# Attention plus token/channel mixer on one core: leftover tokens on all 128 rows, and a scheduler with two transfer queues and new priorities

## The chip, the cores and the metric

The kernel runs on one core of a Trainium2 chip. The metric is the device time of one execution in microseconds (us), the median of three runs. Five engines work in parallel, each on its own list of instructions, in order: PE (TensorE, matrix products), DVE (VectorE), ACT (ScalarE), POOL (GpSimd) and SP (SyncE, which here only issues DMA transfers). ACT issues transfers too. Engines wait for each other through semaphores.

## The reference, cut to what matters

```python
# batch 4, 8 heads, 576 tokens, head size 64; mixer: 576 tokens, 512 channels
scores = q @ k.T / 8 + bias            # bias: per head, from log1p(|i-j|) / log1p(max(i,1)) through
                                       # a hidden layer of 32: relu(x @ w1 + b1) @ w2
attn   = exp(scores - max); attn /= sum(attn) + 1e-9
x      = attn @ v                      # laid out [batch, 576 tokens, 512 channels]
u      = x + (relu(x.T @ w_tok1) @ w_tok2).T       # mixing over tokens, 576 -> 256 -> 576
out    = u + relu(u @ w_ch1) @ w_ch2               # mixing over channels, 512 -> 1536 -> 512
```

## The kernel before

A "unit" is one pair of heads of one batch: 16 units, each 128 channels wide. The 576 query tokens of a unit are cut into four chunks of 128 and 64 **leftover** tokens, which are the fifth chunk (`c == NCH`, `NCH` is 4). In the fifth chunk both heads stand in one tile, head 0 in rows 0 to 63 and head 1 in rows 64 to 127.

PE's steps are these. `mm` (L441) makes one of 36 blocks of the bias, with 32 rows out. `sums` (L474) are 8 small products over v. Per unit there are then nine score products (`scores`, L666, which contract over 64 rows, q by k; the leftover one has 64 rows in and 64 out), nine `flip` transposes (L703), five `back` products (L746 to L748, probabilities by v, in three terms of half precision, 30 instructions), and the token mixer `mix1` (L796 to L798) and `mix2` (L805 to L807), 30 instructions each. After the units come 60 products `chan1` (L968 to L970) and 54 `chan2` (L998 to L1000) of the channel mixer.

In the fifth chunk `back` loads weights of 64 columns for each head, `w[h]`, and writes both heads into the same 64 rows `r`: rows 0 to 63 for an even batch, 64 to 127 for an odd one. The leftover tokens of a unit are therefore a 64 x 128 piece of the tile `x`. `mix1` contracts over these 64 rows in its fifth part (`p = r`), twice (t = 0 and 1); `mix2` makes their result as a product with 64 columns of weights (`slice(512, S)`), at its end.

Between these steps: DVE adds the bias to scores and takes the maximum (`biased`, L670), ACT takes the exponential (L684), flipped blocks are split into two half-precision numbers by ACT (`flip_hi`, L706) and DVE (`flip_lo`, L710), the rest is split by ACT and POOL and turned by a DMA transpose (L722, issued by SP). There are two score buffers (`pair`) and four other PSUM buffers (`bank`). Weights are stored as 64-bit words and are decoded piece by piece (`decode`, L548): DVE, POOL, ACT, DVE.

The order on every engine is not written by hand. Each step is added to a `Plan` with a cost per engine and a due time, made of `BASE`, `TICK` and the table `DUE`; `order()` (L178) picks the engine that can begin first and on it, among the steps that could begin within `SLACK`, the one with the earliest due time. Transfers go to SP's list ("D") or to ACT's ("Q"), and the planner knows one common wire on which they follow each other.

Of the kernel before, what the change touches and what calls it, by code (L numbers as in the profile page):

```python
# [36 lines left out]
TICK = 2.35  # L37
BASE = 67.64
# [16 lines left out]
DUE = {'blk': 29.05,  # L55
       'blkn': 0.67,
       'rect': -81.27,
       'bmm': -146.83,
       'over': -7.76,
       'put': -41.17,  # L60
       'bl': -22.15,
       'bln': 15.56,
       'sums': -79.57,
       'sumsn': 0.87,
       'meas': -52.82,
       'measn': -1.79,
       'measw': 98.18,
       'measwn': 6.48,
       'amax': 56.12,
       'scales': 48.16,  # L70
       'scalet': -63.64,
       'scalec': -167.78,
       'fill': 239.74,
       'fill1': 213.34,
       'tok': 90.83,
       'tokn': 2.6,
       'dec1': 47.92,
       'dec2': -2.25,
       'dec3': -65.12,
       'dec4': 33.12,  # L80
       'dec5': -14.78,
       'load_k': -23.79,
       'load_q': 70.61,
       'load_v': -135.93,
       'prep_k': -68.51,
       'prep_kl': -48.97,
       'prep_q': 82.92,
       'prep_ql': 1.69,
       'prep_v': -126.84,
       'prep_vh': -4.6,  # L90
       'prep_vl': 125.82,
       'scores': 26.19,
       'biased': 82.41,
       'top': 2.07,
       'exp': -41.11,
       'hi': -98.5,
       'lo': -23.53,
       'flip': 29.87,
       'fliphi': 24.58,
       'flip2': 1.74,  # L100
       'fliplo': 11.27,
       'turn': -7.48,
       'back': -24.67,
       'norm': 83.98,
       'mix0': -57.52,
       'mix1': 39.31,
       'relu': -78.51,
       'mix2': -80.52,
       'mix2b': -120.9,
       'store': 48.6,  # L110
       'w1': 22.4,
       'w1n': 11.84,
       'U0': -13.72,
       'U0n': -3.2,
       'U1n': -19.84,
       'U1': -42.9,
       'U2': 133.32,
       'Un': 3.09,
       'U3': 35.03,
       'U4': 250.78,  # L120
       'u1': -106.99,
       'u2': -102.94,
       'u3': 58.75,
       'u4': 8.97,
       'u5': 73.75,
       'G': 114.15,
       'G0': 71.27,
       'G0n': 7.22,
       'g1': -6.35,
       'g2': 90.55,  # L130
       'ur': 190.4,
       'w2m': 20.95,
       'w2mn': 5.39}
# [9 lines left out]
class Step:  # L143
# [5 lines left out]
    def __init__(self, on, due, do, take, free, use, port):  # L149
        key = next(iter(on))  # L150
        self.wire, self.gate = (on[key] if key in "DQX" else 0.0), key == "X"
        on = {"Q": {"A": 0.1}, "X": {"D": 0.0}, "D": {"D": 0.0}}.get(key, on)
# [7 lines left out]
class Plan:  # L160
# [5 lines left out]
    def add(self, on, due, do, after=(), take=(), free=(), use=(), port=False):  # L166

        s = Step(on, due, do, take, free, use, port)
        for p in after:
            if p is not None:  # L170
                p.next.append(s)
                s.left += 1
        for h in free:
            h.users += 1
        self.steps.append(s)
        return s

    def order(self):  # L178
        room = {k: [(0.0, i) for i in range(n)] for k, n in self.rooms.items()}
        at = {"V": 6.9, "A": 6.8, "P": 4.3, "T": 8.0, "D": 2.1, "-": 0.0}  # L180
        made = wire = port = 0.0
# [10 lines left out]
        while len(out) < len(self.steps):  # L192
            best = None
            for e, steps in ready.items():
                first, can = None, []
                for s in steps:
                    t = max(at[e], s.ready, *(h.busy[0] + (0.0 if h.busy[1] == e else 0.15) for h in s.bank))
# [23 lines left out]
            cost = s.on[e]  # L221
            s.start, s.engine = t, e
            if s.wire:
                made = max(made, t + 0.07) + 0.62
# [25 lines left out]
def attention_mixer(ctx, tc, qT, kT, v, cst, lg, ident, wt1, wt2, wc1, wc2, out, dump=None):  # L250
# [67 lines left out]
    def wire(kind, cost):  # L318

        return {QUEUE.get(kind, "D"): cost}  # L320
# [799 lines left out]
```

## Time and profile before

| | us |
|---|---|
| three runs | 712.43, 710.39, 712.82 |
| median | 712.43 |
| span of the profiled execution | 709.6 |
| PE busy in it | 660.5 |
| DVE busy | 469.2 |
| ACT busy | 375.0 |

The span runs from the first to the last instruction; the median run is 2.8 us longer than the profiled span. The execution falls into three stretches: the bias blocks with the first unit, up to about 105 us; the other 15 units, up to about 435; then the channel mixer. The last product ends at about 704.8.

How to read a time line: "start, duration, engine, line, operation, out<-in, shape". Matrix products overlap in PE's pipeline, so the cost of one is the distance from its start to the next one's start. A shape such as 64*128 on PE is the rows by columns of the weights.

### The profile page before, as it was taken

Reading aid. Unit: us, or ns where it says so; the run is one execution under the profiler, and the core shown is the slowest. Engines: PE = TensorE matmul, PEld = TensorE weight load, DVE = VectorE, ACT = ScalarE, POOL = GpSimd, SP = SyncE. Lnnn points to the kernel's source line nnn. Section 1 sums busy time; section 2 is a strip of 40 time slices with the busy share of each in tenths; the row PEclk is TensorE's granted clock in tenths of the full one; section 3 lists DMA queues with packets and bytes.
Section 4 is the critical chain, followed back from the end, with each engine's and each line's share of the span. In section 5 each row is a group of like instructions: output and inputs, shape, how many; then the busy total and the mean of one; then the engine's idle time right before and its main releaser. Section 6 shows DMA issues by size and latency. Waiting matters only on the chain. (4 is left out here: it accounts for less than half of the span.)

```text
span 709.6 us, 16671 instructions
## 1 busy us (share of the span) xinstructions
PE 660.5 (93%) x6612; PEld 391.8 (55%) x6612; DVE 469.2 (66%) x1164; ACT 375.0 (53%) x726; POOL 162.9 (23%) x226
## 2 busy tenths in 40 slices
PE   5776779999999999999999999999999999999997
PEld 2322246676667767776767776444444444446443
DVE  5788788987889999999898777579851022112110
ACT  4667769766787787777877653345531022012010
POOL 0121025332354544453323100013430000000000
PEclk9999999999999999999999999999999999999999
DMA  9878867889756596644452248967623220121021
GB/s 337 332 253 284 280 232 224 245 232 242 237 153 181 132 260 182 177 122 115 135 117 61 49 99 213 296 178 183 181 55 120 60 59 1 29 62 29 19 85 31
DMA packets 86814, 111.42 MB, mean 157 GB/s; under 512 B 46928, under 2 KB 56400, under 8 KB 86736
## 3 DMA queue, kind: packets, MB, share of 16 engines
q1 hardware_dynamic: 72048, 70.90, 35.6%
q10 hardware_dynamic: 14688, 39.46, 17.5%
q8 instruction: 52, 0.85, 0.5%
q14 instruction: 26, 0.21, 0.1%
HBM read 80.31 MB, written 20.05 MB: 141 GB/s over the span
## 5 line engine op out<-in xcount | busy, mean ns | idle before, releaser
L666 PE MATMUL pair<-kk,qq 64*128 64x288 f32 (+1 forms) x640 | 107.6, 454 | 8.6 <-DVE mx L670 5.9
L684 ACT ACTIVATE z<-z,mx 128x576 f32<-128x576 f32 x144 | 110.3, 775 | 6.4 <-DVE mx L691 2.6
L670 DVE CUSTOM_DVE_ANT_0 z<-pair,slots 128x576 f32<-128x576 f32 x144 | 108.4, 757 | 7.6 <-PE pair L666 6.2
L710 DVE TENSOR_TENSOR t2a<-bank,t2a 128x512 f16<-128x512 f32 x144 | 98.3, 687 | 16.4 <-ACT t2a L706 16.0
L706 ACT ACTIVATE t2a<-bank 128x512 f16<-128x512 f32 x144 | 84.4, 588 | 42.3 <-PE bank L703 35.6
L703 PE MATMUL bank<-id,z 128*128 128x128 f32 x576 | 92.7, 285 | 4.6 <-ACT z L684 2.9
L1009 DVE SCALAR_TENSOR_TENSOR o<-bank,crow,ur 128x512 f32<-128x512 f32 x18 | 13.5, 751 | 104.2 <-PE bank L1000 104.2
L703 PEld LDWEIGHTS bank<-id,z 128*128 128x128 f32 x576 | 60.8, 141 | 36.8 <-issue 13.6
L746 PE MATMUL bank<-vh,t2a 128*128 128x65 f16 (+1 forms) x704 | 75.7, 196 | 0.7 <-ACT t2a L706 0.7
L746 PEld LDWEIGHTS <-t2a 128*128 128x128 f16 (+1 forms) x704 | 65.0, 99 | 19.6 <-issue 12.3
L747 PE MATMUL bank<-vl,t2a 128*128 128x64 f16 (+1 forms) x704 | 75.0, 193 | 0.0
L748 PE MATMUL bank<-vh,t2a 128*128 128x65 f16 (+1 forms) x704 | 74.6, 194 | 0.0
L968 PE MATMUL bank<-slots 128*128 128x384 f16 (+1 forms) x192 | 67.8, 353 | 0.8 <-DVE t2a L710 0.8
L323 POOL TENSOR_TENSOR p<-z,p 128x128 f16<-128x128 f32 x80 | 36.6, 459 | 138.1 <-ACT p L308 111.5
L970 PE MATMUL bank<-slots 128*128 128x384 f16 (+1 forms) x192 | 67.7, 353 | 0.0
L969 PE MATMUL bank<-slots 128*128 128x384 f16 (+1 forms) x192 | 67.7, 353 | 0.0
L747 PEld LDWEIGHTS <-t2a 128*128 128x128 f16 (+1 forms) x704 | 65.8, 101 | 1.0 <-issue 0.8
L748 PEld LDWEIGHTS <-t2a 128*128 128x128 f16 (+1 forms) x704 | 65.9, 100 | 0.1
L441 PE MATMUL pair<-slots 128*32 128x288 f32 x576 | 48.5, 455 | 14.6 <-ACT slots L447 13.6
L425 DVE TENSOR_SCALAR slots<-slots 128x576 f32<-128x576 f32 x108 | 51.9, 548 | 15.1 <-PE pair L441 14.9
L666 PEld LDWEIGHTS pair<-kk,qq 64*128 64x128 f32 (+1 forms) x640 | 42.8, 175 | 33.8 <-issue 12.4
L990 ACT ACTIVATE ur<-ur,sc 128x512 f32<-128x512 f32 x18 | 13.0, 720 | 79.2 <-DMA ur<-um 65.1
(171 smaller groups left out, 1404.5 us busy)
## 6 DMA issues: line engine op xcount, KB each, us to landing
raw<-wc SPq DMA_DIRECT2D x48, 512.0 KB, 4.4
bd<-slots ACTq DMA_DIRECT2D x36, 288.0 KB, 4.0
kk<-kT ACTq DMA_DIRECT2D x16, 576.0 KB, 5.1
qq<-qT ACTq DMA_DIRECT2D x16, 576.0 KB, 5.9
slots<-bd SPq DMA_DIRECT2D x16, 576.0 KB, 6.1
tv<-v ACTq DMA_DIRECT2D x16, 320.0 KB, 3.6
slots<-v SPq DMA_DIRECT2D x8, 640.0 KB, 11.6
um<-x SPq DMA_DIRECT2D x16, 256.0 KB, 3.4
```

The costliest lines, as they stand in the source:

```text
L666: PE.matmul(out=o[:, n, 0:i], lhsT=qq[w, q0:q0 + m], rhs=kk[w, k0:k0 + i], start=True, stop=True)
L670: V.tensor_tensor_reduce(out=st["z"][z.i][:, o].rearrange("p (n j) -> p n j", n=2), in0=pairs[ph.i][:, :, 0:i], in1=(bias_m[hp][:, c, h, : ...
L684: A.activation(out=zz, in_=zz, func=ACTF.Exp, bias=mx_t[z.i][:, 2 + h:3 + h], scale=0.125)
L703: PE.transpose(banks[tb.i][:, n * 128:(n + 1) * 128], st["z"][z.i][:, 512 * i + n * 128:512 * i + (n + 1) * 128], id32)
L706: A.activation(out=st["t2a"][h.i][:, 0:4].rearrange("p n q -> p (n q)"), in_=banks[tb.i], func=ACTF.Copy)
L710: V.tensor_tensor(out=x[:, 512:1024], in0=banks[tb.i], in1=x[:, 0:512], op=ALU.subtract)
L746: PE.matmul(out=o, lhsT=lh, rhs=vh[:, n, 0:D + 1], start=(i == 0), stop=False)
L747: PE.matmul(out=ps[q, h, 0:D], lhsT=lh, rhs=vl[:, n, :], start=False, stop=False)
L748: PE.matmul(out=o, lhsT=ll, rhs=vh[:, n, 0:D + 1], start=False, stop=(i == 4))
L968: PE.matmul(out=ps[:, 0:n], lhsT=w[0][:, c], rhs=uh[:, c], start=(c == 0), stop=False)
L969: PE.matmul(out=ps[:, 0:n], lhsT=w[0][:, c], rhs=ul[:, c], start=False, stop=False)
L970: PE.matmul(out=ps[:, 0:n], lhsT=w[1][:, c], rhs=uh[:, c], start=False, stop=(c == 3))
```

## The change

First, the leftover tokens. `back` uses all 128 columns of the fifth chunk's weights for both heads and writes 128 rows; the useful part is block-diagonal (rows 0 to 63 with head 0's channels, rows 64 to 127 with head 1's), and only these two blocks are copied into `x`, whose other blocks stay zero. `mix1` contracts over all 128 rows, and `mix2` makes 128 columns: the second weights of the token mixer get their last 64 columns twice (640 instead of 576). On DVE the leftover normalisation and the leftover sum become two instructions of 64 x 64 where there was one of 64 x 128, and the leftover result of a unit is stored by two transfers of 64 x 64.

Second, the planner. It has two transfer queues ("A" and "D") that each keep their order and share bandwidth (`HALF`), with a work time, a lag and an issue time for each kind of transfer; steps on PE have a `mode`, and a change of mode costs `DRAIN`; some PE costs are lower. Third, `DUE`, `TICK` and `BASE` have other values throughout, so all engines get another order.

```diff
-TICK = 2.35
-BASE = 67.64
+DRAIN = 0.095
+HEAD, HALF, AHEAD = 1.2, 0.445, 2.0
+DMA = {"put": (1.06, 1.62, 0.35), ... "store_l": (0.56, 1.4, 1.0), "turn": (1.22, 1.56, 1.2), ...}
+ROWS64, ROWS64X2, COLS32 = ("64x128", 0.1), ("64x64", 0.1), ("128x32", 0.1)
+TICK = 4.659
+BASE = 5.791
-DUE = {'blk': 29.05,
+DUE = {'blk': -592.583,
...
+                    if e == "T" and s.mode != mode:
+                        t = max(t, at[e] + DRAIN)
...
             if s.wire:
-                made = max(made, t + 0.07) + 0.62
-                wire = max(wire, made + (0.65 if e == "D" else 0.78)) + s.wire
-                s.end = wire + 0.94
+                o = "D" if e == "A" else "A"
+                first = max(till[e], t + HEAD)
+                both = max(0.0, min(till[o] - first, s.wire / HALF))
+                till[e] = first + s.wire + both * (1.0 - HALF)
+                till[o] += both * (1.0 - HALF)
+                s.end = till[e] + s.lag - HEAD
...
                     if c < NCH:
-                        q = slice(0, 128)
                         blk = [[(n, n) for n in range(5)], [(n + 1, n) for n in range(4, 9)]]
-                        w = [slice(0, 128)] * 2
                     else:
-                        q = r
                         blk = [[(n + 5 * h, n) for n in range(5)] for h in range(2)]
-                        w = [slice(0, 64), slice(64, 128)]
...
-                            PE.matmul(out=o, lhsT=lh, rhs=vh[:, n, 0:D + 1], start=(i == 0), stop=False)
+                            PE.matmul(out=o, lhsT=th[t], rhs=vh[:, n, 0:D + 1], start=(i == 0), stop=False)
...
+                    elif c == NCH:
+                        for h, w in enumerate(half):
+                            V.tensor_scalar(out=xo[w, 0, h], in0=ps[w, 0, h, 0:D], scalar1=rc[w, 0, h], scalar2=None, op0=ALU.mult)
...
-                        p = slice(0, 128) if c < 4 else r
-                        PE.matmul(out=ps[:, t], lhsT=w1h[p, c, w], rhs=xh[p, c], start=(c == 0), stop=False)
+                        PE.matmul(out=ps[:, t], lhsT=w1h[:, c, w], rhs=xh[:, c], start=(c == 0), stop=False)
...
-                for o, w in [(ps[:, s], slice(s * 128, (s + 1) * 128)) for s in range(4)] + [(pl, slice(512, S))]:
+                for o, w in [(ps[:, s], slice(s * 128, (s + 1) * 128)) for s in range(4)] + [(pl, slice(512, 640))]:
...
+            def mixed_left(e):
+                for h, w in enumerate(half):
+                    o = x()[w, 4, 64 * h:64 * h + 64]
+                    V.scalar_tensor_tensor(out=o, in0=banks[b1.i][w, 256 + 64 * h:320 + 64 * h], scalar=c_tm[w], in1=o, op0=ALU.mult, op1=ALU.add)
+
+            def store_left(e):
+                for h, w in enumerate(half):
+                    ENG[e].dma_start(out=u_l[b // 2][r, hp * 128 + 64 * h:hp * 128 + 64 * h + 64], in_=x()[w, 4, 64 * h:64 * h + 64])
```

Three places show how the order moves. On PE, at the border of unit 1 and unit 2 (`pair` is a score buffer, `kk` and `qq` the keys and queries, a score of the fifth chunk is the one with 64x320; a row with `id32` is a flip). Before:

```order
L703 MATMUL bank2_68<-id32_73,z2_122 128x128 x4
L666 MATMUL pair0_64<-kk1_107,qq1_108 128x288 x2
L703 MATMUL bank3_69<-id32_73,z2_122 128x128 x4
L666 MATMUL pair1_65<-kk1_107,qq1_108 64x320 x4
L703 MATMUL bank0_66<-id32_73,z3_124 128x128 x4
L666 MATMUL pair0_64<-kk2_109,qq2_110 128x288 x2
L666 MATMUL pair1_65<-kk2_109,qq2_110 128x288 x2
```

The same part of a unit now, in unit 1:

```order
L691 MATMUL pair0_64<-kk1_107,qq1_108 128x288 x2
L691 MATMUL pair1_65<-kk1_107,qq1_108 128x288 x2
L728 MATMUL bank2_68<-id32_73,z2_122 128x128 x4
L691 MATMUL pair0_64<-kk1_107,qq1_108 128x288 x2
L691 MATMUL pair1_65<-kk1_107,qq1_108 64x320 x4
L728 MATMUL bank1_67<-id32_73,z2_122 128x128 x4
```

Scores stand more often side by side: the 144 score steps formed 129 groups of neighbours and form 109 now (of which 25 of two, 2 of three and 2 of four; before 11 of two and 2 of three).

On ACT, in the bias stage, early in the program (L423 is one rectified line of a bias block, L447 copies a finished block out of `pair`, `bd` is that block's transfer to memory, `ds` belongs to the decoding of a token weight). Before:

```order
L423 ACTIVATE slots<-slots 128x576
L452 DMA bd_134<-slots 128x576
L423 ACTIVATE slots<-slots 128x576
L560 ACTIVATE ds<-raw_82 128x512
L447 ACTIVATE slots<-pair_64,slots 128x576
L452 DMA bd_134<-slots 128x576
L447 ACTIVATE slots<-pair_65,slots 128x576
L452 DMA bd_134<-slots 128x576
```

Now, at the same blocks:

```order
L447 ACTIVATE slots<-slots 128x576
L471 ACTIVATE slots<-pair_64,slots 128x576
L447 ACTIVATE slots<-slots 128x576
L476 DMA bd_134<-slots 128x576
L471 ACTIVATE slots<-pair_65,slots 128x576
L476 DMA bd_134<-slots 128x576
L447 ACTIVATE slots<-slots 128x576
L471 ACTIVATE slots<-pair_64,slots 128x576
```

The decoding step stood ahead of the fifth block's copy and stands behind the eighteenth now; rectified lines and copies alternate. Elsewhere in this stage, the first two bias blocks stand ahead of the first `sums` on PE (before, the first `sums` came first), the transfers of k and q of unit 0 are issued ahead of ACT's first work, two token weights are loaded ahead of the v that `sums` reads, and 13 steps of unit 0 stand ahead of the last bias block on PE (before: 6).

On DVE, at the end of the decoding of the second channel weights (`w2l` is the low half of one of their 12 pieces, `mrut`, `ua` and `ul` belong to the preparation of later token blocks, `o` is an output block). Before:

```order
L556 TENSOR_SCALAR dc_6693<-raw_6690 128x512
L571 SCALAR_TENSOR_TENSOR w2l<-dm_6691,sc,w2h 128x512
L561 SCALAR_TENSOR_TENSOR dc_6693<-dm_6692,dc_6693 128x512
L571 SCALAR_TENSOR_TENSOR w2l<-dm_6692,sc,w2h 128x512
L1009 SCALAR_TENSOR_TENSOR o_6906<-bank_66,crow,ur_6903 128x512
```

Now:

```order
L968 TENSOR_SCALAR crow<-mrut_165,sc 128x1
L322 TENSOR_REDUCE mrut_166<-ua_6712 128x1
L295 TENSOR_SCALAR mrut_166<-mrut_166 128x1
L296 TENSOR_SCALAR mrut_166<-mrut_166 128x1
L313 TENSOR_SCALAR mrut_166<-mrut_166 128x1
L968 TENSOR_SCALAR crow<-mrut_166,sc 128x1
L1038 TENSOR_SCALAR crow<-crow,sc 128x1 x2
L981 SCALAR_TENSOR_TENSOR ul_6711<-ua_6709,mrut_165,uh_6710 128x512
L981 SCALAR_TENSOR_TENSOR ul_6714<-ua_6712,mrut_166,uh_6713 128x512
L595 SCALAR_TENSOR_TENSOR w2l<-dm_6705,sc,w2h 128x512
L1041 SCALAR_TENSOR_TENSOR o_6930<-bank_67,crow,ur_6927 128x512
```

The twelfth piece's low half now stands behind the preparation of two later token blocks, and on PE the first `chan2` step that reads pieces 9 to 12 is the seventh `chan2` step (before: the ninth).

## Rows read from the trace of the kernel before

**Rows 1.** The page, engines over the span: busy us, share, instructions.
```profile
PE 660.5 (93%) x6612; PEld 391.8 (55%) x6612; DVE 469.2 (66%) x1164; ACT 375.0 (53%) x726; POOL 162.9 (23%) x226
```
**Rows 2.** Stretches: us; PE, PEld, DVE, ACT, POOL busy (instructions); PEclk, DMA share, GB/s.
```profile
8.30:105.00 96.70, 72.09 (x828) 33.77 (x828) 73.87 (x177) 64.14 (x103) 15.21 (x20) 0.93 0.81 287
105.00:435.00 330.00, 319.35 (x4467) 230.47 (x4467) 292.18 (x768) 243.92 (x516) 123.72 (x169) 1.00 0.61 165
435.00:709.60 274.60, 269.05 (x1320) 127.59 (x1318) 99.83 (x209) 64.33 (x106) 22.77 (x24) 1.00 0.35 98
```
**Rows 3.** Time line of PE, one mix1 and the step behind it.
```profile
207.97 0.22 PE L797 MATMUL bank<-xl,wt1h 128*128 128x128 f16 x1
...
208.53 0.22 PE L798 MATMUL bank<-xh,wt1l 128*128 128x128 f16 x1
208.68 0.23 PE L796 MATMUL bank<-xh,wt1h 64*128 64x128 f16 x1
...
210.00 0.20 PE L746 MATMUL bank<-vh,t2a 128*128 128x65 f16 x1
```
**Rows 4.** Time line of PE, the mix2 that follows and the step behind it.
```profile
211.82 0.22 PE L806 MATMUL bank<-hl,wt2h 128*128 128x128 f16 x1 [0.21 <-DVE hl L816]
...
213.04 0.22 PE L807 MATMUL bank<-hh,wt2l 128*128 128x128 f16 x1
213.19 0.24 PE L805 MATMUL bank<-hh,wt2h 128*64 128x128 f16 x1
...
213.65 0.20 PE L746 MATMUL bank<-vh,t2a 128*128 128x65 f16 x1
```
**Rows 5.** Time line of PE, back of a full chunk, flip, score, back of leftovers, flip.
```profile
217.09 0.20 PE L746 MATMUL bank<-vh,t2a 128*128 128x65 f16 x1
...
218.01 0.63 PE L703 MATMUL bank<-id,z 128*128 128x128 f32 x4
218.57 0.76 PE L666 MATMUL pair<-kk,qq 64*128 64x288 f32 x4
219.26 0.22 PE L746 MATMUL bank<-vh,t2a 128*64 128x65 f16 x1
...
220.32 0.66 PE L703 MATMUL bank<-id,z 128*128 128x128 f32 x4
```
**Rows 6.** Time line of PE, three score steps side by side (two merged in one row).
```profile
204.42 1.24 PE L666 MATMUL pair<-kk,qq 64*128 64x288 f32 x8
206.05 0.76 PE L666 MATMUL pair<-kk,qq 64*128 64x288 f32 x4 [0.38 <-DVE mx L670]
```
**Rows 7.** Waits of PE from 105 to 435 us: total, times, longest.
```profile
PE pair L666 <- DVE mx L670: 5.9, 7, 1.7
```
**Rows 8.** Waits of PE from 8.3 to 105 us.
```profile
PE pair L441 <- ACT slots L447: 13.6, 15, 2.2
PE bank L474 <- DMA slots<-v: 8.3, 1, 8.3
```
**Rows 9.** Groups of DVE instructions by shape: count, busy us, mean ns, idle before.
```profile
L821 DVE SCALAR_TENSOR_TENSOR x<-bank,sc,x 64x128 f32<-64x128 f32 x16 | 5.5, 345 | 0.3
L780 DVE TENSOR_TENSOR x<-bank,rc 64x128 f32<-64x128 f32 x16 | 4.6, 286 | 0.3
L767 DVE TENSOR_SCALAR rc<-bank 64x2 f32<-64x2 f32 x16 | 2.5, 154 | 0.8 <-PE bank L748 0.6
```
**Rows 10.** Busy time in one slice of 20 us, columns as in rows 2.
```profile
300.00:320.00 20.00, 20.00 (x314) 14.97 (x311) 19.09 (x46) 15.64 (x33) 10.60 (x13) 1.00 0.42 110
```
**Rows 11.** Transfers by issuing queue: count, size, median us from issue to landing.
```profile
ua<-um SPq DMA_DIRECT2D x9, 256.0 KB, 4.0
uT<-uh SPq DMA_TRANSPOSE x4, 3.2
```
**Rows 12.** Time line, the twelfth piece of the second channel weights, and its reader.
```profile
531.21 0.75 DVE L571 SCALAR_TENSOR_TENSOR w2l<-dm,sc,w2h 128x512 f16<-128x512 f32 x1 [2.09 <-ACT w2h L564]
...
531.22 0.38 PE L998 MATMUL bank<-w2h,slots 128*128 128x512 f16 x1
```

More of the change, by code (lines that the diff above doesn't have):

```diff
@@ L54 @@
       'lo': {'P': (2.32, 11.69)}}
-DUE = {'blk': 29.05,
[L56 to L133, printed above, removed]
@@ new lines @@
+DUE = {'blk': -592.583,
+       'blkn': 13.236,
+       'rect': -728.881,
+       'bmm': 340.411,
+       'over': 11.335,
+       'put': -525.596,
+       'bl': 500.43,
+       'bln': -195.426,
+       'sums': 121.838,
+       'sumsn': 566.503,
+       'meas': -1364.245,
+       'measn': -663.302,
+       'measw': 1040.532,
+       'measwn': 17.694,
+       'amax': 1085.724,
+       'scales': -264.266,
+       'scalet': -628.831,
+       'scalec': -464.634,
+       'fill': -68.983,
+       'fill1': -1737.522,
+       'tok': 27.022,
+       'tokn': -6.894,
+       'dec1': 58.698,
+       'dec2': 162.039,
+       'dec3': 524.544,
+       'dec4': -1436.632,
+       'dec5': -2556.755,
+       'load_k': 49.487,
+       'load_q': 1250.555,
+       'load_v': -2116.276,
+       'prep_k': -704.678,
+       'prep_kl': 131.787,
+       'prep_q': -861.596,
+       'prep_ql': 1260.292,
+       'prep_v': -359.143,
+       'prep_vh': 1250.124,
+       'prep_vl': -1026.9,
+       'scores': 135.604,
+       'biased': 487.707,
+       'top': 457.116,
+       'exp': 772.211,
+       'hi': -36.273,
+       'lo': 184.792,
+       'flip': -537.037,
+       'fliphi': 778.858,
+       'flip2': -1303.835,
+       'fliplo': 545.789,
+       'turn': 87.262,
+       'back': -885.383,
+       'norm': -159.117,
+       'mix0': -1382.7,
+       'mix1': -2289.411,
+       'relu': -411.29,
+       'mix2': -1240.874,
+       'mix2b': -404.587,
+       'store': 921.234,
+       'w1': 2210.742,
+       'w1n': 80.985,
+       'U0': 1606.419,
+       'U0n': 61.875,
+       'U1n': -1030.813,
+       'U1': -353.576,
+       'U2': -715.42,
+       'Un': -609.944,
+       'U3': 1554.027,
+       'U4': 243.375,
+       'u1': 77.861,
+       'u2': 2158.847,
+       'u3': 101.146,
+       'u4': -806.841,
+       'u5': 56.065,
+       'G': 444.142,
+       'G0': 524.339,
+       'G0n': -2.212,
+       'g1': 619.041,
+       'g2': -412.512,
+       'ur': 498.05,
+       'w2m': -278.659,
+       'w2mn': 209.85}
@@ L164, in __init__, with add @@
         self.rooms, self.steps = rooms, []
-    def add(self, on, due, do, after=(), take=(), free=(), use=(), port=False):
-        s = Step(on, due, do, take, free, use, port)
+    def add(self, on, due, do, after=(), take=(), free=(), use=(), port=False, mode=None):
+        s = Step(on, due, do, take, free, use, port, mode)
         for p in after:
@@ L316, in share, with wire @@
         return {e: 0.09 + (x - 0.09) * k if isinstance(x, float) else (0.09 + (x[0] - 0.09) * k, x[1]) for e, x in on.items()}
-    def wire(kind, cost):
-        return {QUEUE.get(kind, "D"): cost}
+    def wire(kind, part=1.0, at=None):
+        work, lag, issue = DMA[kind]
+        return {at or QUEUE.get(kind, "D"): (work * part, lag, issue)}
     def less(e, o, x, y):
@@ L628, in unit @@
             r = slice(64 * (b % 2), 64 * (b % 2) + 64)
+            half = [slice(0, 64), slice(64, 128)]
             def load(tiles, h, x):
@@ L944, in turn @@
                 return do
-            s = add(wire("u", 0.85), t0, lambda e: ENG[e].dma_start(out=buf(0), in_=u_of(tk)), after=[*ok, *(s for b in bs for hp in range(HP) for s in stored[hp, b])], take=[h])
+            s = add(wire("u"), t0, lambda e: ENG[e].dma_start(out=buf(0), in_=u_of(tk)), after=[*ok, *(s for b in bs for hp in range(HP) for s in stored[hp, b])], take=[h])
             s = add({"V": 1.3}, t0 + DUE["u1"], scale, after=[s])
```

111 lines of the change are left out of this document (63 added, 48 removed).

## The prediction, made before the result was known

> **What bounds the kernel now.** I read the page's busy shares first: PE works 660.5 of 709.6 us, DVE, the next, 469.2 [rows 1]. Then the busy time by stretch [rows 2], because a mean over stages hides which of them is full. From 435 us to the end PE is busy 269.05 of 274.6, and what is left is the output behind the last product: full. From 105 to 435 us it is busy 319.35 of 330.0, so 10.6 us are lost; DVE stands beside it with 292.18 (89%). In the first stretch, from the first product at 8.3 us to 105, PE is busy 72.09 of 96.7, DVE 73.87, ACT 64.14: no engine is full there, and the time goes into waiting for each other. PE's clock was granted at 0.93 of full in that stretch and at 1.00 in the two others. So from 105 us on, a microsecond taken off PE's own work is nearly a microsecond off the end, unless another engine then makes PE wait; before that, the order of the steps decides. The waits of PE say the same: from 105 to 435 the only one over 2 us in sum is for the bias addition on DVE that frees a score buffer, 5.9 us [rows 7]; before 105, 13.6 us for ACT's copy of bias blocks, and the start itself, 8.3 us [rows 8].
>
> **What the leftover edit takes off PE.** The price is not in how many products there are (30 per step before and after) but in the gaps where the shape of the weights changes. In mix1, products of one shape start 0.056 us apart ((208.53 - 207.97)/10); from 128*128 to 64*128 weights the gap is 0.15 [rows 3]. There are four such borders in a mix1 (into and out of the 64-row part, twice). From the second product at 207.97 to the next step at 210.00 it takes 2.03 us; 29 products at 0.056 would take 1.62. That is 0.41 a unit, 6.6 us for 16 units. In mix2 the border is at its last part, 64 columns wide, 213.04 to 213.19, and again at its end: 211.82 to 213.65 is 1.83, 29 products are 1.62, so 0.21 a unit and 3.4 us [rows 4]. With 128 columns in place of 64 the price of one product stays as it is, since the 64-row and 128-row products already start at the same distance. The leftover back takes 219.26 to 220.32, 1.06 us; a full one 217.09 to 218.01, 0.92 [rows 5]. Of these 0.14, 0.09 is the border at its end and 0.05 lies inside; the 0.05 goes everywhere, 0.8 us. A border goes only where the neighbour also has full weights; where a score stands beside it, there is a border still. In the order before, 19 of the 32 neighbours are not scores: 1.8 us. Together 2.6. The leftover edit is worth 6.6 + 3.4 + 2.6 = 12.6 us of PE, nearly all of it beyond 105 us.
>
> The Trainium skill, TensorEngine Tiling (Array Packing), Key Properties, says that changing the tiling mode drains the engine; the 0.15 beside 0.056 is what that costs here. The same page, When to Use Tiling, would have weights of at most 64 columns kept in column tiles, which speaks against this edit: by it a leftover back should cost half of a full one, and the edit would add about 0.4 us a unit, 7 us in all. The row shows 1.06 beside 0.92, so here the narrow tiles ran one after the other and bought nothing, and I take the row.
>
> **What the new order takes off PE.** A score contracts over 64 rows, so a group of scores has a border at both ends. Alone, a score takes 0.69 until its successor (218.57 to 219.26) and lasts 0.76 [rows 5]; two side by side last 1.24 [rows 6], so the second adds 0.48 where a lone one takes 0.69: 0.2 saved for each group that is merged into another. 129 groups become 109: 20 x 0.2 = 4.0 us. Against it, the bias products (32 columns) stand in 20 groups instead of 14 among the others: 6 x 0.2 = 1.2 us more. Net 2.8 us. PE's work falls by 12.6 + 2.8 = 15.4 us.
>
> **What comes back as waiting, 105 to 435 us.** Two score buffers mean that the third score in a row waits for DVE's addition: 0.38 us in the trace [rows 6]. Two groups of three and two of four replace two of three; the fourth waits as well, so four waits more, some 2 us. DVE gets more work: the leftover sum is now two instructions for one of 345 ns, the leftover scaling two for one of 286 ns [rows 9]. The halves are not in the trace. At most they cost as much as the whole, at least nothing over it: 0 to 0.63 us a unit, 0 to 10.1 us of DVE. An instruction of the same 64 rows with 2 columns takes 154 ns [rows 9], so much of the price is fixed; halfway between 154 and the whole, two halves cost about 0.3 us more, 5 us in all. PE does not wait for these (the sum goes to a store, the scaling to a token mixer that has chunks of other work ahead of it). DVE would then be busy 297 of some 318 us, 93%. Is that too much? In the slice from 300 to 320 us DVE is busy 19.09 and PE 20.00 of 20 [rows 10]: both can be this full at once when the order fits. I take 3 us of added waiting in this stretch, with -3 (half of the 5.9 goes) and +8 as ends.
>
> **The first stretch.** 13 steps of unit 0 instead of 6 stand ahead of the last bias product. Seven steps are about 7 us of PE work that would move from behind the bias stage into its idle time. If all of it fits, 7 us are won; DVE and ACT get the work around these steps earlier too and each has a quarter or more of the stretch free [rows 2]. ACT's copies no longer stand behind the decoding of a token weight, and the copies are what PE waits for, 13.6 us [rows 8]. Against it: k and q of unit 0 and two token weights are fetched ahead of, or beside, the first tables and v, and the first product waited 8.3 us for a transfer [rows 8]; two bias products can go ahead of that one now. I take 3 us won, with 7 won and 5 lost as ends. The 16 more stores (two of 64 x 64 for one) are off PE's path, and nobody reads them before the channel mixer; I cost them at nothing.
>
> **The channel mixer.** The 60 and 54 products are the same; I cost their order at nothing, with one exception. Before, the twelfth piece of the second weights was written at 531.21, and the step that reads pieces 9 to 12 began at 531.22 [rows 12], reaching the twelfth piece some 2 us later: little to spare. Now that step is the seventh of its kind, not the ninth, and the piece's low half stands on DVE behind two token blocks whose loads (4.0 us) follow four transposes (3.2 us) that wait for the end of chan1 on SP [rows 11]. The transposes queue behind each other (an estimate of 5 to 8 us until the buffers are free), the load takes 4.0, and DVE and ACT some 4 for the two blocks: the piece is ready 13 to 16 us after chan1 ends, and the seventh step begins 6 x 2.6 = 15.6 us after it, and reads the piece 2 us later. I take 1 us of wait, from 0 to 4.
>
> **The sum.** 709.6 - 15.4 + 3 - 3 + 1 = 695.2 us of span; the median lies 2.8 over the span: **698.0 us**. Ends of the unknown terms: -3 - 7 + 0 below, + 8 + 5 + 4 above; that they all fall on one side is unlikely.
>
> **Rivals.**
> (a) PE's work falls, and half of it comes back: with PE ahead, DVE's lateness decides in the stretch from 105 to 435. For it: DVE at 93%, one buffer wait already of 1.7 us [rows 7]. Against: the slice in rows 10. Added waits at the upper end, 8 instead of 3, and nothing won in the first stretch: 698 + 5 + 3 = 706. Chance 0.17.
> (b) The order is better than I can count: the first stretch wins its 7 us, and waits fall by 3: 698 - 4 - 6 = 688; a point below that if the twelfth piece costs nothing. Chance 0.13.
> (c) It doesn't do what it says: the gaps of 0.15 belong to the start of another sum in PSUM, not to the shape of the weights, and stay. Then 12.6 us stay with PE: 710.6, no change. Against: at 208.53 to 208.68 the sum goes on and only the shape changes, and in mix2 22 products in a row, in which three new sums begin, take 213.04 - 211.82 = 1.22 us, 0.055 each [rows 3, 4]. Chance 0.05.
> (d) Slower: neighbouring scores wait for DVE each time, not only the third. There are 29 groups of more than one score. If the addition comes late, as in the longest wait of 1.7 us, 29 x 1.7 = 49 us would be lost; to eat the gain of 14.4 us a mean of 0.50 us a group is enough, and at 0.7 the time is 712.4 - 14.4 + 20.3 = 718. For it: DVE's list is long and in order. Against: two scores side by side ran in 1.24 us without a wait [rows 6], and all buffer waits together are 5.9 us with 13 such groups. Chance 0.06.
> The forecast itself, 690 to 704, has 0.59.
>
> **How the numbers follow.** The range should leave out 2 in 10: from 688 (b at its likeliest) to 708 (a, with some over) it holds the forecast, most of (a), half of (b). A change of 0.3%, 2.1 us, is about what a measurement can tell here: same is 710.3 to 714.6. Faster gets the forecast, (a) and (b), 0.89, less a little of (a) that may reach 711: 0.87; same gets (c) and that rest: 0.06; slower gets (d) and what I did not think of: 0.07.
>
> **What would show each step right or wrong.** In the time line after: mix1 and mix2 with all starts 0.056 apart and the next step behind them without a gap of 0.15, about 1.67 us each. The leftover back at 0.92. PE's work from 105 us on down by some 14 us; the stretch up to the end of the units shorter by about as much. PE's waits for the bias addition: 5 to 9 us is my case, 15 and more is (a) or (d). The last bias product should start at 82 to 90 us and unit 1's first score by 100. PE should have hardly a wait behind the last unit; one for the second weights, before the seventh chan2 step, of over 4 us would make my exception too small. I am wrong if gaps of 0.15 stay, if PE's work falls and its idle time grows by as much, or if the first stretch grows by over 5 us.

## The result, and the profile after

| | before | after |
|---|---|---|
| median of four runs, us | 712.16 | 705.11 |
| lowest to highest | 710.39 to 712.82 | 700.63 to 706.63 |
| span of the profiled execution | 709.6 | 704.5 |
| start of unit 1's first score | 103.3 | 102.7 |
| start of the last leftover back | 426.1 | 411.4 |
| start of the first chan2 step | 510.5 | 505.1 |

The ratio is 0.9894, 95% interval 0.986 to 0.9929: 7 us faster, half of the 14.4 that I forecast. First the edit itself, in PE's time line: a mix1, a mix2 and the last leftover back, the second product of each mixer, the first of the back, and the first of the step behind each. (Columns: start, us, engine, line, operation, tiles, weights rows*columns, out.)

```profile
220.59 0.22 PE L820 MATMUL bank<-xl,wt1h 128*128 128x128 f16 x1
...
222.15 0.22 PE L821 MATMUL bank<-xh,wt1l 128*128 128x128 f16 x1
222.20 0.28 PE L728 MATMUL bank<-id,z 128*128 128x128 f32 x1
...
226.14 0.22 PE L829 MATMUL bank<-hl,wt2h 128*128 128x128 f16 x1
...
227.76 0.19 PE L766 MATMUL bank<-vh,t2a 128*128 128x65 f16 x1
...
411.36 0.19 PE L766 MATMUL bank<-vh,t2a 128*128 128x65 f16 x1
...
412.27 0.33 PE L1000 MATMUL bank<-slots 128*128 128x384 f16 x1
```

From the second product to the next step mix1 now takes 1.61 us (2.03 in [rows 3]) and mix2 1.62 (1.83 in [rows 4]); the leftover back takes 0.91 (1.06 in [rows 5]). The gaps of 0.15 are gone, as forecast. The stretches of the changed kernel (columns as in [rows 2]):

```profile
8.30:105.00 96.70, 73.47 (x851) 35.55 (x852) 79.51 (x191) 67.15 (x112) 19.58 (x27) 0.93 0.93 311
105.00:435.00 330.00, 316.20 (x4523) 235.94 (x4520) 297.18 (x803) 245.61 (x523) 119.44 (x164) 1.00 0.61 170
435.00:704.50 269.50, 261.03 (x1246) 122.52 (x1244) 92.78 (x186) 60.96 (x101) 21.41 (x24) 0.99 0.30 86
```

The waits of PE that answer to [rows 7] and [rows 8], from 105 to 435 us, then from 8.3 to 105 (total, times, longest):

```profile
PE pair L691 <- DVE mx L695: 8.0, 14, 1.4
...
PE pair L465 <- ACT slots L471: 11.1, 11, 1.8
PE pair L465 <- DVE slots L449: 8.9, 1, 8.9
```

The wait for the bias addition rose from 5.9 to 8.0, inside the 5 to 9 that I called my case. In the last stretch PE lost 8.5 us where before it lost 5.6, and the clock is at 0.99. All its waits there, and the place of the first in its time line:

```profile
PE bank L300 <- DVE mch L319: 2.6, 1, 2.6
PE bank L306 <- DVE dgc L305: 1.0, 1, 1.0
...
451.55 0.38 PE L1002 MATMUL bank<-slots 128*128 128x512 f16 x1
454.53 0.27 PE L300 MATMUL bank<-id,mch 128*1 128x128 f32 x1 [2.60 <-DVE mch L319]
455.76 0.58 PE L306 MATMUL bank<-dgc,ones 1*128 1x1 f32 x2 [0.96 <-DVE dgc L305]
456.27 0.61 PE L1000 MATMUL bank<-slots 128*128 128x512 f16 x1
456.67 0.63 PE L1001 MATMUL bank<-slots 128*128 128x512 f16 x1
457.10 0.63 PE L1002 MATMUL bank<-slots 128*128 128x512 f16 x1
...
462.31 0.38 PE L1000 MATMUL bank<-slots 128*128 128x512 f16 x1
462.53 0.38 PE L1001 MATMUL bank<-slots 128*128 128x512 f16 x1
```

PE waited 2.6 us for the scale of the second channel weights (`w_scale`, which needs the maximum over all twelve pieces, `mch`), and behind it products of 512 columns start 0.43 us apart, not 0.215, until 461.8: the clock was granted at 1.2 GHz instead of 2.4, and one chan1 step took 5.1 us instead of 2.6. From the last leftover back to the first chan2 step 5.4 us are lost, nearly all of it here. Each piece is fetched, then measured by DVE; the last instruction for the maximum, in the kernel before, then in the changed one:

```profile
460.89 0.15 DVE L295 TENSOR_SCALAR mch<-mch 128x1 int32<-128x1 int32 x1
...
454.32 0.15 DVE L319 TENSOR_SCALAR mch<-mch 128x1 int32<-128x1 int32 x1
```

The maximum is there 6.6 us earlier than before. But PE came to it at 461.7 before, 0.6 us behind it, and comes now at 451.9, 9.8 us earlier: 2.6 us too early.

The loss and gain by place, in the two profiles: to unit 1's first score -0.6 us; from there to the last leftover back -10.2 (chan1 steps there, four before and two now, taken out at 1.95 us each); to the first chan2 step +5.4; from there to the end +0.3. Sum -5.1, the difference of the spans.

### The profile page after: what moved, and what is told of

Same layout as the page of the kernel before. It is cut to its first block, busy times and chain, and to the rows that moved or that the text cites. A ratio compares the mean times of both kernels' runs of the same rounds, so it can differ in the third digit from the quotient of the medians.

```text
span 704.5 us, 16767 instructions
## 1 busy us (share of the span) xinstructions
PE 650.7 (92%) x6612; PEld 394.0 (56%) x6612; DVE 471.8 (67%) x1187; ACT 375.4 (53%) x735; POOL 161.5 (23%) x226
## 4 chain that ended last, share of the span: by engine, by line
PE 55%; DVE 18%; DMA 11%; ACT 6%; issue 5%; POOL 3%; SPq 1%; ACTq 1%; POOLq 0%; DVEq 0%
PE bank L1031 7%; PE bank L1032 7%; PE bank L1030 7%; PE pair L691 6%; PE bank L1000 5%; PE bank L1001 5%; PE bank L1002 5%; DVE z L695 5%; PE bank L728 4%; DMA t<-p 4%; DVE t2a L735 4%; PE pair L465 2%; DMA raw<-wc 2%; DMA bd<-slots 2%; PE bank L766 2%
## 5 line engine op out<-in xcount | busy, mean ns | idle before, releaser
L731 ACT ACTIVATE t2a<-bank 128x512 f16<-128x512 f32 x144 | 84.7, 588 | 30.1 <-PE bank L728 23.9
L766 PE MATMUL bank<-vh,t2a 128*128 128x65 f16 x704 | 74.6, 195 | 0.6 <-DVE x L804 0.4
L767 PE MATMUL bank<-vl,t2a 128*128 128x64 f16 x704 | 74.5, 192 | 0.0
L768 PE MATMUL bank<-vh,t2a 128*128 128x65 f16 x704 | 74.0, 193 | 0.2 <-DVE t2a L735 0.2
L766 PEld LDWEIGHTS <-t2a 128*128 128x128 f16 x704 | 65.1, 97 | 7.2 <-issue 6.7
L1000 PE MATMUL bank<-slots 128*128 128x384 f16 (+1 forms) x192 | 68.9, 359 | 0.0
L465 PE MATMUL pair<-slots 128*32 128x288 f32 x576 | 47.9, 448 | 22.7 <-ACT slots L471 11.1
L1001 PE MATMUL bank<-slots 128*128 128x384 f16 (+1 forms) x192 | 68.8, 358 | 0.0
L1002 PE MATMUL bank<-slots 128*128 128x384 f16 (+1 forms) x192 | 68.7, 358 | 0.0
L767 PEld LDWEIGHTS <-t2a 128*128 128x128 f16 x704 | 65.1, 99 | 1.9 <-issue 0.9
L768 PEld LDWEIGHTS <-t2a 128*128 128x128 f16 x704 | 65.1, 97 | 0.3 <-DVE t2a L735 0.3
L449 DVE TENSOR_SCALAR slots<-slots 128x576 f32<-128x576 f32 x108 | 53.6, 558 | 7.4 <-PE pair L465 7.3
```

The lines of the kernel that those rows point to most:

```text
L731: A.activation(out=st["t2a"][h.i][:, 0:4].rearrange("p n q -> p (n q)"), in_=banks[tb.i], func=ACTF.Copy)
L766: PE.matmul(out=o, lhsT=th[t], rhs=vh[:, n, 0:D + 1], start=(i == 0), stop=False)
L767: PE.matmul(out=ps[:, h, 0:D], lhsT=th[t], rhs=vl[:, n, :], start=False, stop=False)
L768: PE.matmul(out=o, lhsT=tl[t], rhs=vh[:, n, 0:D + 1], start=False, stop=(i == 4))
L1000: PE.matmul(out=ps[:, 0:n], lhsT=w[0][:, c], rhs=uh[:, c], start=(c == 0), stop=False)
L1001: PE.matmul(out=ps[:, 0:n], lhsT=w[0][:, c], rhs=ul[:, c], start=False, stop=False)
```

## The experiments

In the table, "units" is the time from the start of unit 1's first score to that of the last leftover back, less the chan1 steps in it. "PE work" adds up the steps of that stretch, each at the distance from its start to the next one's where nothing was waited for (the lower fifth of all steps of its kind with the same kind of neighbour, over all profiles); "waiting" is the rest. Both are estimates: with the lower tenth in place of the lower fifth "PE work" comes out some 1.5 to 2.5 us smaller in every kernel, and "waiting" larger.

**Edit and order apart.** The two kernels have the same 2817 steps, so each one's code can be run with the list of steps, engines and buffers that the other's planner gave:

```diff
     def order(self):
...
+        for w in ORDER.split():
+            n, e, *bufs = w.split(",")
+            s = self.steps[int(n)]
+            s.engine = e
+            for h, i in zip(s.take, bufs):
+                h.i = int(i)
+            out.append(s)
```

> The leftover edit alone: the changed kernel's code, its steps in the order, on the engines and in the buffers of the kernel before. My theory: the edit takes 12.6 us of PE work away (mix1 6.6, mix2 3.4, leftover back 2.6) and 1 to 4 us come back as waits, since the halves cost DVE 0.49 us a unit by the changed kernel's rows (283 and 278 ns for each of two halves, 286 and 345 ns for the whole before): 712.2 - 12.6 + 1 to 4 = 700 to 704, and no wait of over 1 us at the second weights' scale. Rival: the old order was planned for longer token mixers, so more than half of the gain turns into waits: 706 or more.

> The new order alone: the code of the kernel before (64-row leftovers), its steps in the order, on the engines and in the buffers of the changed kernel. My theory: fewer score groups give 2.8 us, the wait for the second weights' scale and the low clock behind it cost some 5 us, the first stretch gives nothing: 712.2 - 2.8 + 5 = 713 to 716, so the new order by itself is no gain. Rival: the order is worth its 2.8 us and more, and only the changed kernel's shorter mixers bring PE too early to the scale: then PE, 10 us later there, waits under 1 us for it, and the time is 706 to 710.

> The changed kernel once more, its instructions in the same order on every engine, so that it stands on one chip beside the runs below. My theory: 703 to 706 as before; the wait of 2 to 3 us for the second weights' scale is there again, with a stretch at half clock behind it, and unit 1's first score comes at 99 to 100, as in the three runs with the new order since, not at 102.7: that was a second stretch at half clock in that one profile. Rival: 102 to 103 is what this kernel does, and the three others had some other luck.

| kernel | median, us | ratio, interval | units | PE work | waiting |
|---|---|---|---|---|---|
| before | 712.2 to 713.4 | 1 | 315.0 | 298.3 | 16.7 |
| edit alone, old order | 707.51 | 0.9921 (0.9893 to 0.9948) | 315.9 | 287.2 | 28.7 |
| order alone, old code | 705.85 | 0.9889 (0.9857 to 0.9921) | 310.5 | 296.3 | 14.2 |
| both | 705.11 | 0.9894 (0.986 to 0.9929) | 304.8 | 284.1 | 20.7 |
| both, again | 702.53 | 0.9873 (0.9839 to 0.9906) | 305.4 | 284.1 | 21.3 |

Both my theories fell, and both rivals held (the order's 705.85 lies just under its 706 to 710). The edit takes 11.1 us of PE work out of the units in the old order, and in the profiled execution 12.0 come back as waiting there; its median is lower by 5.6 us, not by 12.6. The 12.0 is too much for the usual execution: the profiled one took 711.0 us, the longest of ten, and in it the clock was granted at 0.99 from 105 to 435 us, which takes some 3 us away (an estimate: 0.01 of 330), and PE waited 2.2 us for one turned block. The stretch, and that wait (columns as in [rows 2] and [rows 7]):

```profile
105.00:435.00 330.00, 313.81 (x4468) 231.13 (x4469) 293.81 (x798) 243.27 (x515) 123.88 (x169) 0.99 0.62 165
...
PE bank L766 <- DMA t<-p: 3.2, 2, 2.2
```

The new order alone is as fast as the whole change. It needs little PE work less (2.0) and waits less (2.5), brings the first stretch forward, and reaches the scale of the second weights at 455.8 with 0.2 us of waiting. On top of it the edit takes 12.2 us of PE work out of the units, shortens them by 5 to 6 us in these two profiles (by 0.6 to 5.7, in the mean 3.6, over all six profiles that have the same code and order up to the scale: their units take 304.8 to 309.9 us), and gives 1 to 4 of that back at the scale (85.5 us from the last leftover back to the first chan2 step with the order alone, 89.8 and 86.5 with both; two chan1 steps of 1.95 us taken off, to compare with the 84.4 of before). The gains don't add: 5.6 and 7.9 alone (on one chip), 7 to 9 together.

The repeat had a wait of 1.2 us at the scale, shorter than I expected; the stretch at half clock followed it again. Unit 1's first score came at 102.1, as the rival had it. Over the profiles of all kernels here with the new order it comes at 98.9 to 102.7, in the mean at 100.8; over those with the old order at 102.8 to 103.6, mean 103.2. So the first stretch is 2.4 us shorter in the mean, and the profile of the result stood at the late end.

**The scale of the second weights.** Two edits of the changed kernel. One moves `w_scale` in the list behind two more chan1 steps; the other leaves it where it is and gives PE useless work in place of the wait (this edit is the one shown):

```diff
-            m = mch[:, 12:13]
+            m, w, x = mch[:, 12:13], wch[0, "h"], uT[1][0][:, 0, 0:512]; [PE.matmul(out=banks[hw.i], lhsT=w[:, i, 0:128], rhs=x, start=True, stop=True) for i in range(12)]
```

> The changed kernel with one step moved: the scale of the second weights stands behind two more chan1 steps of its block (5.2 us of PE work) instead of ahead of them, on PE and on DVE. My theory: the 2.6 us wait for the measured weights and the stretch at half clock behind it (some 2.8 us) go and nothing else becomes late: the changed kernel's time less 5, about 700. Rival: what the scale is needed for becomes late in its turn (the decoding of the second weights on DVE, ACT and POOL), and the first chan2 steps wait: 703 to 706.

> The changed kernel with 12 products of 128 x 512 (2.6 us of PE work at full clock, their sums overwritten) ahead of the second weights' scale, where PE waited 2.6 us. It tells what the low clock behind the scale comes from. My theory: it comes from PE standing idle there; with PE busy the clock stays at full, the next chan1 step takes 2.6 us and not 5.1, and the time is the changed kernel's less 2.8: about 702.3, though 2.6 us of useless work are in it. Rival: the clock falls for another cause (it stood at 0.9 earlier in the run too), the step still takes some 5 us: 705, no change.

> The kernel with the late scale once more, on another chip: its ratio to the kernel before was 0.9798, while two kernels that are this one with one edit more each stood at 0.984 on their chip, where the changed kernel stood at 0.987. My theory: the step's move is worth 3 to 5 us and the edits on top nothing: 0.981 to 0.984, 699 to 701. Rival: 0.9798 is right, and both edits on top of it cost 2 us or more: 697 to 699.

Moved: 699.07 us, ratio 0.9798 (0.9763 to 0.9833); again, on another chip, 701.95, 0.9805 (0.9768 to 0.9842). With useless work: 702.46, 0.9844 (0.9799 to 0.9889), as my theory had it; but the changed kernel's repeat took 702.53, so what tells here is the clock and the place, not the time. The stretch from 452 to 464 us in the changed kernel, its repeat, with useless work, and moved (columns as in [rows 2]):

```profile
452.00:464.00 12.00, 8.51 (x26) 3.55 (x27) 5.64 (x23) 1.16 (x2) 0.64 (x1) 0.72 0.40 131
...
452.00:464.00 12.00, 10.40 (x42) 4.63 (x43) 5.50 (x28) 1.47 (x4) 0.65 (x1) 0.86 0.33 118
...
452.00:464.00 12.00, 11.04 (x56) 5.33 (x55) 6.31 (x26) 2.48 (x5) 0.65 (x2) 1.00 0.26 101
...
452.00:464.00 12.00, 10.79 (x54) 5.26 (x53) 8.71 (x33) 3.88 (x7) 2.43 (x3) 1.00 0.47 168
```

The granted clock is 0.72 after a wait of 2.6 us, 0.86 after one of 1.2, and 1.00 where PE had work or came later. The first chan2 step stood at 505.1 and 501.8 in the changed kernel; it stands at 500.0 with useless work and at 497.7 moved (501.1 in the repeat, where unit 1 began 2.2 us later and the units took 0.8 longer). Nothing became late behind the moved scale: from the last leftover back to the first chan2 step it takes 83.8 us (84.2 in the repeat), counted as above, against 89.8 and 86.5 in the two profiles of the changed kernel, 86.5 with the useless work, and 84.4 before. So the 5.4 us were the wait and the clock behind it, both: busy products took back 3.3 of them, the move all. The step's move is worth about 0.8% of the time; the two ratios of 0.980 agree, and by the ratio the repeat's rival, not its theory, had the number; its median of 701.95 lies above both ranges.

**DVE's two halves.** In the changed kernel the leftover scaling and sum are two instructions each (count, then busy us and mean ns):

```profile
L802 DVE TENSOR_SCALAR x<-bank,rc 64x64 f32<-64x64 f32 x32 | 9.1, 283 | 0.7
L848 DVE SCALAR_TENSOR_TENSOR x<-bank,sc,x 64x64 f32<-64x64 f32 x32 | 8.9, 278 | 0.5
```

A half costs as much as the whole in the case of the scaling (286 in [rows 9], there as a TENSOR_TENSOR) and four fifths of it in the other (345). That is 0.49 us a unit more, 7.9 in all. One instruction over all 128 rows does the same work if the off-diagonal reciprocals are made next to nothing (a mask `m` of 1 and 1e25 in the instruction ahead of the reciprocal):

```diff
+                    V.tensor_scalar(out=rc, in0=ps[:, :, :, D:D + 1], scalar1=GUARD, scalar2=None, op0=ALU.add) if c < NCH else V.scalar_tensor_tensor(out=rc, in0=ps[:, :, :, D:D + 1], scalar=GUARD, in1=m, op0=ALU.add, op1=ALU.mult)
...
+                o = x()[:, 4]
+                V.scalar_tensor_tensor(out=o, in0=banks[b1.i][:, 256:384], scalar=c_tm, in1=o, op0=ALU.mult, op1=ALU.add)
...
-                    elif c == NCH:
-                        for h, w in enumerate(half):
-                            V.tensor_scalar(out=xo[w, 0, h], in0=ps[w, 0, h, 0:D], scalar1=rc[w, 0, h], scalar2=None, op0=ALU.mult)
```

> The leftover edit in the order of the kernel before, with the leftover scaling and sum on DVE as one instruction each, as in the run beside it. With two each, the edit had 11 us less PE work in the units and 12 us more waiting. My theory (DVE sets the pace): 5 to 8 us come off 707.5: 700 to 703. Rival (the order sets the pace: PE now comes to each wait earlier and waits for chains that are as long as before): 706 to 708.

> The kernel with the late scale, and the leftover scaling and the leftover sum on DVE each as one instruction over all 128 rows instead of two over 64 (the reciprocals of the off-diagonal blocks are made zero with a mask in the instruction ahead). By the rows of the changed kernel that takes 2 x 283 + 2 x 278 - 286 - 345 = 491 ns of DVE a unit away, 7.9 us in all. My theory: in the units DVE sets the pace together with PE, and the edit's gain on PE came back as waits for DVE; so 4 to 7 us come off: 692 to 695 where the late scale alone had 699.1. Rival: the waits come from the order of the steps and the two score buffers, not from how much DVE has to do: 698 to 700.

In the old order: 702.46 us, 0.9853 (0.9829 to 0.9878), against 0.9921 with the halves, and the waiting in the units falls from 28.7 to 19.7 us in the two profiles. Of these 9.0 us some belong to the long execution above (its clock, its one wait); by the ratios one piece is worth 4.8 us, for the 7.9 that DVE has less to do. There the theory holds: the halves ate about half of the edit. And with DVE's work as it was, 11.1 us less PE work brings the kernel 10.5 us under the one before by the ratio, 8.1 of them in the units: most of it comes through. In the new order with the late scale: 701.02 us, 0.9837 (0.981 to 0.9865), the waiting 22.9 us against 23.1 and 23.9 in the two profiles with halves. There the theory falls; the time lies a little above the rival's 698 to 700. Over the profiles with this code and order the waiting goes from 20.7 to 25.8 us with halves and from 19.5 to 22.9 in one piece, too near to tell. The waits of PE for the bias addition and for turned blocks, from 103 to 410 us with halves and from 103 to 412 us in one piece:

```profile
PE pair L691 <- DVE mx L695: 7.3, 13, 1.6
PE bank L766 <- DMA t<-p: 4.5, 7, 1.4
...
PE bank L766 <- DMA t<-p: 5.5, 6, 1.8
PE pair L691 <- DVE mx L695: 5.2, 9, 1.2
```

Here the wait for turned blocks takes part of what the wait for the bias addition gives. But in the other profile of the late scale, with halves, the two are 5.4 and 2.7 us: they vary as much from one execution to another as between the versions, so a shift from one to the other is not shown.

**What sets the pace in the units.** Both on the kernel with the late scale; one leaves out 36 us of PE work (mix1 is shown, mix2 goes the same way), the other 38 us of DVE's:

```diff
-                        PE.matmul(out=ps[:, t], lhsT=w1h[:, c, w], rhs=xh[:, c], start=(c == 0), stop=False)
-                        PE.matmul(out=ps[:, t], lhsT=w1h[:, c, w], rhs=xl[:, c], start=False, stop=False)
-                        PE.matmul(out=ps[:, t], lhsT=w1l[:, c, w], rhs=xh[:, c], start=False, stop=(c == 4))
+                        PE.matmul(out=ps[:, t], lhsT=w1h[:, c, w], rhs=xh[:, c], start=(c == 0), stop=(c == 4))
...
-                        V.tensor_tensor(out=x[:, 512:1024], in0=banks[tb.i], in1=x[:, 0:512], op=ALU.subtract)
+                        V.tensor_tensor(out=x[:, 512:768], in0=banks[tb.i][:, 0:256], in1=x[:, 0:256], op=ALU.subtract)
```

> The kernel with the late scale, and in both products of the token mixer only the high parts: 20 of 30 products of each are left out (the outputs are less exact). That is 40 x 16 x 0.056 = 36 us less PE work in the units, and nothing less on DVE, ACT and the queues. It asks what PE work is worth there. My theory: the edit's 12 us gave only some 4 in the new order, so PE is not what sets the pace in the units: a third to a half comes off, 12 to 18 us, 681 to 687. Rival (my prediction's reading, PE sets the pace): 28 us or more, 671 or less.

> The kernel with the late scale, and DVE's subtraction for the low part of a flipped block (684 ns, 144 times) on half of its columns; the other half of the low part stays zero (the outputs are less exact). By the row for 256 columns (420 ns) that takes 0.26 x 144 = 38 us off DVE, nearly all in the units, and nothing off PE. My theory: in the new order DVE still sets the pace together with PE, and what one instruction instead of two halves did not show was too small or lay in the wrong place; of 23 us of PE waiting in the units 8 to 14 go: 685 to 691. Rival (transfers and the order of the steps set it): under 4 us, 695 to 699.

Less PE work: 700.35 us, 0.9811 (0.978 to 0.9843). Less DVE work: 695.19 us, 0.9742 (0.9714 to 0.9769). The late scale beside them on the same chip: 701.95. The ratio of the late scale there is 0.9805. So 36 us of PE work are worth nothing by the ratios (some 4 us by the far ends of the intervals) and 1.6 us by the medians, far less than even my theory allowed, and 38 us of DVE's 4.5 us by the ratios and 6.8 by the medians: less than the 8 to 14 of my theory, more than the rival's 4, though the time lies in the rival's 695 to 699. The stretch from 105 to 410 us: late scale, less PE, less DVE.

```profile
105.00:410.00 305.00, 288.69 (x4273) 218.63 (x4272) 276.88 (x744) 234.61 (x504) 117.26 (x161) 1.00 0.59 162
...
105.00:410.00 305.00, 268.30 (x3737) 192.88 (x3738) 277.96 (x749) 233.80 (x505) 116.29 (x160) 0.98 0.60 163
...
105.00:410.00 305.00, 292.78 (x4357) 223.56 (x4356) 252.80 (x761) 236.09 (x509) 117.63 (x162) 1.00 0.62 166
```

With 36 us less to do PE is busy 20 us less, and the units take 304.7 us, as in the changed kernel, and 2.5 to 3.3 less than with the late scale (307.2 and 308.0); DVE is as busy as before. With less DVE work the units take 300.7, and PE's waiting falls from 23.9 to 16.6. So by the units it is 3 us for PE's work and 7 for DVE's. In the kernel with less PE work, the longest sums of PE's waits (103 to 410 us) now name DVE nearly everywhere:

```profile
PE pair L691 <- DVE mx L695: 7.1, 12, 2.1
PE bank L766 <- DVE t2a L735: 6.2, 7, 1.6
PE bank L766 <- DMA t<-p: 4.8, 8, 1.1
PE bank L728 <- DVE t2a L735: 3.2, 6, 1.2
PE bank L728 <- DVE x L842: 2.8, 4, 1.4
```

A part of what was saved went to the clock, which was granted at 0.98 in that stretch where it was 1.00 or 0.99 with the late scale: by these figures an estimate of 3 to 6 us of the 36.

**Everything together.** The scale's two products on PE have 1.0 us of waiting for DVE between them (I had taken the 1.8 us from the first to the next step for it); they can stand around a chan1 step.

```diff
+            magnitude(m); half_way = max_exponent(m, 1, "c2", banks[hw.i], True)
...
+            s.do(s.engine); s is plan.steps[2399] and st["rest"]()
```

> The kernel with the late scale, and its two products on PE, between which PE stood 1.8 us for DVE, set around a chan1 step: the first behind the last step of its block, the second one step later. My theory: PE is the bound there, so 1 to 2 us come off 699.1: 697 to 698. Rival: the scale being 2.6 us later still, the decoding of the second weights becomes late and the first chan2 steps wait: 699 to 701.

> Late scale, its two products around a chan1 step, and the leftover scaling and sum in one instruction each, all together: the version that should beat both kernels if the single gains add up. My theory: the last two give nothing that can be measured in this order, so 698 to 701, as the late scale alone beside it. Rival: they add up, 1.8 us at the scale and some 5 in the units: 692 to 695.

Split: 701.39 us, 0.9835 (0.9808 to 0.9863), over the ranges of both its theory and its rival, though no chan2 step became late. All three, as its theory had it: 698.51 us, 0.9795 (0.9765 to 0.9825). From the last leftover back to the first chan2 step these two take 82.8 and 82.9 us, against 83.8 and 84.2 with the late scale alone: the split gives about 1 us at its place, which the times can't show. The version with all three beats both kernels: 14 to 15 us under the one before, some 6 under the changed one. Nearly all of that second part is the late scale.

## Why the prediction was right, and why it was only half right

The time of 705.11 lies in the range, and the direction held. It is not the forecast, though: it is the 706 of rival (a), "half of it comes back", to which I gave 0.17. That the number fits so well is partly luck. Rival (a) adds 5 us of waiting between 105 and 435 us and leaves out the 3 of the first stretch. In the profile of the result the span is 9.3 us over my 695.2: 2.2 of them in the units, 2.4 in the first stretch, 4.4 at the scale of the second weights, which (a) does not have, and 0.3 behind it. The offset from span to median took 2.2 back.

**PE's work**: right. The gaps went; the units have 14.2 us less PE work in the traces against 15.4 for the whole kernel in the sum (12.2 of it from the edit in the new order, 2.0 from the order, where I had 12.6 and 2.8).

**"A microsecond taken off PE's own work is nearly a microsecond off the end"**: wrong as a price for the stretch from 105 to 435 us, and this is the step that failed, although in the sum it cost only 2.2 us. I read it from a busy share of 97%. Busy time of overlapping products hides part of the waiting: by the starts of the steps 16.7 us of the 315.0 were waiting even before. In the old order the rule nearly held as long as DVE had no more to do (8 to 10 us for 11.1), and about half of it went when DVE got the halves (5.6 us). In the new order, taken away alone, 36 us of PE work gave at most 3. My reading is that PE and DVE, 97% and 89% full, wait for each other in turn, so that neither alone is the bound. My 3 us of added waiting came out at 4.0 and 4.6 in the two profiles of the changed kernel, and at up to 9.1 over the six with its code and order, although the new order by itself takes 2.5 away.

**DVE's halves**: under-estimated, 5 us for 7.9, since I put a half midway between a 2-column instruction and the whole, and it costs nearly the whole. "PE does not wait for these" was wrong in the old order: there they cost about 5 us by the ratios. In the new order no cost of theirs can be measured.

**The first stretch**: -3 was about right (2.4 in the mean of the profiles); the profile of the result shows 0.6 of it. My signs for it failed there: the last bias product starts at 91.1 us, not at 82 to 90, and unit 1's first score at 102.7, not by 100. And the seven steps (three scores, two flips, two backs) are some 5 us of PE work by [rows 5], not 7.

**The second weights**: right that they would be late, wrong about the place and the size, and the largest single miss of the sum. I followed the second pass of the pieces (decoding, the seventh chan2 step) and found 1 us; that step came without a wait. The first pass, which measures the pieces for the scale, I left out, though it stands earlier on the same queue: PE came 9.8 us earlier to it, and the pieces only 6.6. It cost 5.4 us in one profile and 2.1 in the other, where I had 1.

**From span to median** I added the 2.8 us of before; it was 0.6 here.

What stays open: in the new order neither PE's nor DVE's work alone is worth much. That points to a chain that runs through several engines and SP's turned blocks in the order of the list, but which of its links would have to be moved I did not settle. A list planned anew for the shorter mixers was not tried.

## What to carry to other kernels

A busy share of 97% does not give a price: before costing PE work at its full length, take a large piece of it out and see what the time does, and see what the same change adds to the engine beside it. When an engine is made faster, list everything that it will meet earlier, transfers above all, and look how far each moves with it: the first one that moves less is the new wait. And splitting a small DVE instruction into two halves cost three quarters of a whole one here (491 ns more for two that were split, of 286 and 345 ns).

## What I had not expected of the hardware

A wait of 1.2 to 2.6 us of PE was followed by a stretch at the lower clock in both profiles of the changed kernel (granted 0.86 and 0.72 over 452 to 464 us); 2.6 us of useless products in place of the wait kept it at 1.00 and cost no more than the wait (86.5 us from the last leftover back to the first chan2 step, against 89.8 and 86.5). In the kernel before, PE stood 1 us between the scale's two products as well, without losing the clock; at the scale of the first channel weights in the edit alone, waits of 0.5 and 1.0 us were followed by a granted clock of 0.83 over 186 to 196 us. And executions of one and the same program differ by 6 us in the changed kernel (700.63 to 706.63, the mean granted clock between 0.977 and 0.988) and by 9 in the one with useless work (698.02 to 707.35, 0.984 to 0.996): effects of a few us were better seen in the starts of named steps than in the times.
